# V kept per chunk and copied in one run per partition, with two full copy sets, a reused K buffer and a new order table

## Chip, cores and metric

One core of one Trainium2 chip. The metric is the device time of one launch in microseconds (us). Lower is better. Engines are called as in the profile: PE is the matmul engine, DVE, ACT and POOL are the vector, scalar and GpSimd engines, SP is the one that issues nearly all DMAs of both kernels. Four runs of the kernel before lay between 215.65 and 216.56 us; runs marked slow (over 1.5% above the fastest of the same kernel) are left out of every ratio.

## The reference, cut to what matters

```python
# x: 1 x 2048 x 512 (S x D), H = 32 heads of 16, window of W = 8 keys at distance 2 (dil)
h = layernorm(x) * (1 + ca) + sa                     # sa, ca, ga, sb, cb, gb = silu(c) @ w_mod
q, k, v = split_heads(h @ wqkv)
logits[s, w] = q[s] . k[s - 2 w] * Dh**-0.5          # masked where s - 2 w < 0
o[s] = sum over w of softmax(logits)[s, w] * v[s - 2 w]
x = x + ga * (o @ wo)
h = layernorm(x) * (1 + cb) + sb
h = layernorm(h)                                     # then a two-layer MLP along the sequence
x = x + gb * transpose(gelu(h^T @ w1 + b1) @ w2 + b2)
```

The sequence is handled in five chunks of 2, 4, 4, 4 and 2 tiles of 128 rows. DVE multiplies q by shifted k and the attention weights by shifted v; PE sums the products with narrow 0/1 matrices.

## The kernel before

For the products with V the partition of an operand is (window group w4, head): 32 heads in each of four groups of 32 partitions, group w4 holding V shifted by 2 w4 rows. So V, which lies with (head, quarter of the head's dimensions dq) on its partitions, is copied four times within SBUF, by DMA. The kernel before keeps one V of the whole sequence and copies each chunk quarter by quarter:

```python
v_f = T([P, 4, PAD + S], BF, "v_f")                      # partition = 4 * head + dq
vD_r = ring(5, [P, 4 * (CM + 8)], BF, "vD")              # five buffers of one quarter (NVD = 5)
...
for dhi in range(4):                                     # a quarter
    s_ = _Slot("vd"); vds.append(s_)
    for w4 in range(4):                                  # a window group
        s0 = PAD - 8 - 2 * w4
        def dst(s_=s_, w4=w4):
            return vD_r[s_.i][32 * w4:32 * w4 + 32, 0:4 * (C + 8)].rearrange("p (d s) -> p d s", d=4)
        dma(dst, v_c[dhi::4, :, s0:s0 + C + 8], ...)     # 4 runs of 2 * (C + 8) bytes per partition, on SP
...
# product of quarter dq: waits for the four copies of that quarter
nc.vector.tensor_tensor(pv(), a2sb..., vD_r[s_v.i]..., op=ALU.mult)
```

All these copies, the DMA transposes of the normalised tiles (hT) and all loads are issued by one engine, SP, in the order of a table that is part of the kernel. The modulation rows (ga and so on, spread over all partitions) are made by PE: four matmuls of 512 columns each.

## Time and profile before

| | kernel before |
|---|---|
| median of 3 runs | 216.03 us (215.65 to 216.56) |
| span of the profiled run | 214.4 us |
| first query-key product on DVE | 20.2 us |
| last normalised tile (h3) | 149.1 us |
| DVE idle between these two | 7.5 us |
| PE from the last h3 to the end | the MLP's last 284 matmuls, 61.5 us |

How to read it: between the first product and the last h3 DVE sets the pace, with PE nearly full beside it (busy for 121.4 and 124.6 of 128.9 us); then PE alone (busy for 61.2 of 61.5 us). A microsecond in which DVE idles in the first of these stages moves the end by about one: between the changed kernel and v_quarter_bytes (section 6) this idle time differs by 15.8 us and the time by 15.75. DVE's idle time there is the span of the stage less the union of its instructions. The V copies appear in the list of DMA issues (buffer and source, queue, number of issues, KB of one, median us from issue to landing):

```profile
vD<-v_f SPq DMA_DIRECT2D x48, 130.0 KB, 7.4
...
vD<-v_f SPq DMA_DIRECT2D x32, 66.0 KB, 3.6
```

And the chain of work that ended last, by engine, is PE's:

```profile
PE 73%; DVE 15%; DMA 4%; issue 3%; ACT 1%; POOLq 1%; SPq 1%; DVEq 0%
```

### The profile page before, as it was taken

To read this page: it belongs to the slowest core of one execution; us is meant where nothing else is said; L and a number is where in the kernel's file an instruction comes from. 1 tells how busy PE (TensorE), PEld (TensorE's weight loads), DVE (VectorE), ACT (ScalarE), POOL (GpSimd) and SP (SyncE) were. 2 spreads that over 40 slices of the span, in tenths; PEclk is the share of its full clock that TensorE was granted. 3 is DMA by queue.
4 is the path that set the end of the run, shared out by engine and by line. 5 is a ranking of instruction groups with operands and counts; after the bars stand their busy time and mean duration, and the time that the engine had idled before them with its cause. 6 is when DMAs were issued, how large, how long until landed. Compare 5 with 4: busy or idle time off the path is not lost.

```text
span 214.4 us, 3880 instructions
## 1 busy us (share of the span) xinstructions
PE 201.8 (94%) x1453; PEld 99.9 (47%) x1475; DVE 168.1 (78%) x256; ACT 123.9 (58%) x270; POOL 24.2 (11%) x43
## 2 busy tenths in 40 slices
PE   7599999899999999999999999988999999999992
PEld 7479345335444447443443344333444444444451
DVE  3699999799999999999999789997854445544553
ACT  3548778658789989988857668886852000000000
POOL 6030709100000000000000034034000000000000
PEclk9958999999999999999999999999999999999998
DMA  5999974359999999999999886449879110111011
GB/s 170 355 351 333 206 210 101 90 124 161 148 130 134 134 137 311 134 131 135 223 272 207 220 222 174 127 97 321 203 181 249 49 45 28 54 49 49 24 49 50
DMA packets 54182, 34.24 MB, mean 160 GB/s; under 512 B 18452, under 2 KB 54164, under 8 KB 54164
## 3 DMA queue, kind: packets, MB, share of 16 engines
q1 hardware_dynamic: 54156, 34.00, 74.6%
q8 instruction: 11, 0.18, 0.4%
q14 instruction: 7, 0.06, 0.1%
q10 hardware_dynamic: 8, 0.00, 0.0%
HBM read 22.03 MB, written 2.10 MB: 113 GB/s over the span
## 4 chain that ended last, share of the span: by engine, by line
PE 73%; DVE 15%; DMA 4%; issue 3%; ACT 1%; POOLq 1%; SPq 1%; DVEq 0%
PE psS L238 69%; DVE st L238 4%; DVE h L238 4%; PE psL L238 4%; DVE big L238 4%; DMA xx<-in_A_x_dram 3%; DMA hT<-h 2%; DVE mv L238 1%; POOLq L1082 1%; DVE xx L238 1%; SPq L238 1%; DVE w_qkv L238 0%; ACT lv L238 0%; ACT o_sb L238 0%; ACT k_f L238 0%
## 5 line engine op out<-in xcount | busy, mean ns | idle before, releaser
L238 PE MATMUL psS<-h,wst 128*128 128x512 bf16 x216 | 50.9, 379 | 1.7 <-POOL h L238 1.2
L238 PE MATMUL psS<-hT,w_qkv 128*128 128x512 bf16 (+1 forms) x234 | 47.1, 346 | 1.2 <-DMA hT<-h 0.9
L238 PEld LDWEIGHTS <-wst 128*128 128x128 bf16 x324 | 30.3, 99 | 35.4 <-issue 4.1
L238 PEld LDWEIGHTS <-w_qkv 128*128 128x128 bf16 x282 | 29.8, 114 | 23.7 <-issue 5.8
L238 DVE TENSOR_TENSOR big<-a2sb,vD 128x4096 bf16<-128x4096 bf16 (+1 forms) x20 | 37.0, 1863 | 2.0 <-DMA vD<-v_f 1.5
L238 DVE TENSOR_TENSOR big<-q_sb,k_f 128x4096 bf16<-128x4096 bf16 (+1 forms) x20 | 36.8, 1859 | 0.2 <-ACT k_f L238 0.2
L238 DVE SCALAR_TENSOR_TENSOR h<-psS,bcol,gb_bc 128x512 f32<-128x512 f32 (+1 forms) x17 | 12.2, 719 | 24.6 <-PE psS L238 24.5
L238 ACT ACTIVATE gT<-psS 128x512 bf16<-128x512 f32 x28 | 15.9, 591 | 5.2 <-PE psS L238 5.2
L238 PE MATMUL psS<-gT,big 128*128 128x512 bf16 x83 | 18.2, 379 | 0.1
L238 DVE BATCH_NORM_STATS2 st<-xx 128x6 f32<-128x512 bf16 x21 | 14.2, 675 | 4.2 <-DMA xx<-in_A_x_dram 4.1
L238 PE MATMUL psS<-woq,o_sb 128*128 128x512 bf16 x61 | 16.2, 380 | 0.2
L238 PE MATMUL psS<-gT,wst 128*128 128x512 bf16 (+1 forms) x83 | 15.3, 343 | 0.1
L238 PEld LDWEIGHTS <-big 128*128 128x128 bf16 x116 | 9.2, 98 | 12.3 <-DMA big<-in_w_mod_dram 2.4
L238 ACT ACTIVATE h<-xx,nb,rs 128x512 bf16<-128x512 bf16 x17 | 13.3, 809 | 1.8 <-DVE nb L238 1.7
L238 PEld LDWEIGHTS <-ident 128*128 128x128 bf16 (+1 forms) x146 | 11.1, 110 | 6.8 <-issue 1.7
L238 POOL TENSOR_SCALAR h<-xx,mv,rs 128x512 bf16<-128x512 bf16 x2 | 4.3, 2132 | 87.5 <-DVE xx L238 87.0
L238 ACT ACTIVATE q_sb<-psS,qvb 128x512 bf16<-128x512 f32 (+1 forms) x20 | 11.7, 605 | 4.0 <-PE psS L238 3.9
L238 DVE TENSOR_TENSOR psS<-psS,gT 128x512 f32<-128x512 f32 x14 | 9.2, 695 | 4.6 <-PE psS L238 4.6
L238 ACT ACTIVATE v_f<-psS,qvb 128x512 bf16<-128x512 f32 (+1 forms) x20 | 11.5, 601 | 1.1 <-PE psS L238 0.7
L238 POOL TENSOR_SCALAR h<-xx,rs,nb 128x512 bf16<-128x512 bf16 x7 | 10.3, 1485 | 15.3 <-DMA woq<-in_A_wo_dram 8.6
L238 ACT ACTIVATE k_f<-psS 128x512 bf16<-128x512 f32 x16 | 9.5, 597 | 4.0 <-PE psS L238 3.7
L238 ACT ACTIVATE lv<-mv,epscol 128x1 f32<-128x1 f32 (+2 forms) x25 | 7.3, 292 | 7.9 <-DVE mv L238 5.7
(96 smaller groups left out, 234.9 us busy)
## 6 DMA issues: line engine op xcount, KB each, us to landing
vD<-v_f SPq DMA_DIRECT2D x48, 130.0 KB, 7.4
wst<-in_B_w_dram SPq DMA_DIRECT2D x6, 768.0 KB, 5.6
wst<-in_B_w_dram SPq DMA_DIRECT2D x4, 896.0 KB, 5.8
big<-in_B_w_dram SPq DMA_DIRECT2D x3, 896.0 KB, 6.3
vD<-v_f SPq DMA_DIRECT2D x32, 66.0 KB, 3.6
out_dram<-h SPq DMA_DIRECT2D x15, 128.0 KB, 1.7
xx<-in_A_x_dram SPq DMA_DIRECT2D x3, 512.0 KB, 9.7
gT<-in_w_mod_dram SPq DMA_DIRECT2D x3, 512.0 KB, 9.4
```

The lines of the kernel that those rows point to most:

```text
L238: r = fn(*a, **k)
L1082: with _tile.TileContext(nc) as tc:
```

## The change

The intent: 20 issues of V copies instead of 80, each with one long run for each partition and quarter; V in two buffers of one chunk instead of a whole-sequence tensor (and K's buffer used twice), which frees SBUF; two full sets of copies instead of five quarters; fewer changes between wide and narrow matmuls by a new order table; PE busy with filler matmuls at the start. The modulation rows are made by 64 one-column matmuls, transposed, stored to DRAM and read back to all partitions. Cut to its core:

```diff
-    NVD: int = 5,
+    NVD: int = 2,
...
-    v_f = T([P, 4, PAD + S], BF, "v_f")
+    v_r = ring(2, [P, 4 * (CM + PAD)], BF, "v_sb")
...
-    vD_r = ring(NVD, [P, 4 * (CM + 8)], BF, "vD")
+    vD_r = ring(NVD, [P, 4, 4 * (CM + PAD)], BF, "vD")
...
-        for dhi in range(4):
-            s_ = _Slot("vd")
-            vds.append(s_)
-            for w4 in range(4):
-                s0 = PAD - 8 - 2 * w4
...
-                dma(dst, v_c[dhi::4, :, s0:s0 + C + 8], 32 * 4 * (C + 8) * 2,
...
+        s_ = _Slot("vd")
+        for w4 in range(4):
+            def f_vd(s_=s_, w4=w4):
+                n_ = 4 * (C + PAD) - PAD + 8
+                v_ = v_c[:, 0, PAD - 8 - 2 * w4:PAD - 7 - 2 * w4]
+                nc.sync.dma_start(vD_r[s_.i][32 * w4:32 * w4 + 32, :, 0:n_],
+                                  bass.AP(v_.tensor, v_.offset, [[v_.ap[0][0], P], [1, n_]]))
...
+            dma(lambda scr=scr: scr.rearrange("r (t p) -> (r t) p", p=P), rows, ...)      # rows to DRAM
+            dma(lambda r0=r0, nr=nr: rows_bc[:, r0:r0 + nr, :], ... scratch ...)          # and back, to all partitions
... (new order table; MLP sweeps cut at other tiles; normalisations on other engines)
```

Each product with V now waits for all four copies of its chunk, 2.1 MB in a chunk of four tiles.

## The prediction

> **What bounds the kernel now.** I read the busy shares first, then busy time by stage, then the chain that ended last, then the waits.
>
> ```profile
> PE 201.8 (94%) x1453; PEld 99.9 (47%) x1475; DVE 168.1 (78%) x256; ACT 123.9 (58%) x270; POOL 24.2 (11%) x43
> ...
> PEclk9958999999999999999999999999999999999998
> ```
>
> PE looks full, but the clock line shows two slices at half and 0.8, between 10.7 and 21 us. I therefore cut the span where the work changes: 20.2 us is the first query-key product on DVE, 149.0 us the last normalised tile (h3).
>
> ```profile
> core 0: us, PE busy (x) PEld busy (x) DVE busy (x) ACT busy (x) POOL busy (x), PEclk, DMA share, GB/s
> 2.90:20.20 17.30, 14.61 (x189) 12.88 (x188) 14.05 (x45) 9.41 (x21) 3.34 (x11) 0.80 1.06 339
> 20.20:143.40 123.20, 119.58 (x940) 54.38 (x955) 116.51 (x152) 99.91 (x225) 16.64 (x10) 1.00 0.93 168
> 143.40:149.00 5.60, 4.92 (x23) 2.15 (x23) 4.79 (x13) 3.46 (x10) 2.21 (x2) 1.00 1.05 287
> 149.00:210.50 61.50, 61.22 (x293) 29.05 (x297) 31.81 (x47) 9.88 (x15) 0.00 (x0) 1.00 0.35 93
> ```
>
> From 20.2 to 149 PE and DVE are both nearly full (DVE 121.3 of 128.8 us), so this stage has two bounds. After 149 us only PE matters: 284 matmuls of 512 columns are left (60 of the first MLP layer, 224 of the second), 61.5/284 = 0.2167 us each. What starts the tail is in the timeline:
>
> ```profile
> 146.77 2.17 POOL L238 TENSOR_SCALAR h<-h,mv,rs 128x512 bf16<-128x512 bf16 x1 [3.33 <-ACT rs L238]
> ...
> 148.99 5.34 PE L238 MATMUL psS<-h,wst 128*128 128x512 bf16 x23 [0.60 <-POOL h L238]
> ```
>
> The last normalisations stand on the slow POOL. What the change's title attacks, the shifted copies of V, costs almost nothing in waits; of the DVE's waits (us in total, times, longest):
>
> ```profile
> DVE h L238 <- PE psS L238: 24.5, 16, 2.4
> ...
> DVE big L238 <- DMA vD<-v_f: 1.5, 1, 1.5
> ```
>
> One more loss is hidden inside "busy" PE: changing between full-array and 32-column matmuls.
>
> ```profile
> 57.24 0.38 PE L238 MATMUL psS<-xx,ident 128*128 128x512 bf16 x1
> 57.55 0.62 PE L238 MATMUL psL<-big,group 128*32 128x512 bf16 x8
> 58.09 1.04 PE L238 MATMUL psS<-woq,o_sb 128*128 128x512 bf16 x4
> ```
>
> Four narrow matmuls run abreast, so eight should take 2 x 0.216 = 0.43 us; from start to next start they take 0.54. The plain one before them takes 0.31 instead of 0.216. Over all such groups the median loss is 0.115 us per switch.
>
> [...]
>
> **The change part by part.** The operations below are counted from the built order of both kernels; durations are those of before.
>
> 1. V copies: 80 issues become 20, 8.35 MB become about 8.7 MB. SP issues 60 x 0.606 = 36 us less, but SP bounds nothing. Worth at most the 1.5 us wait. Two full sets of V copies are enough: each set is rewritten two chunks later.
>
> 2. PE work. Removed: 16 matmuls of 512 columns for the modulation rows (3.5 us), 7 re-injections (1.5). Added: 64 one-column matmuls (16 take 0.55, so 2.2), two tiny transposes, one identity matmul (0.2), 90 filler matmuls early, outside the critical work, and a last output tile cut in three rather than two. Mode switches fall from 78 to 48: 30 x 0.115 = 3.5 us. Without fillers PE does about 6 us less. Between the first reduction and the first MLP matmul the old PE sum is 69.1 us, and before really took about 69 us there: PE was the bound. The new sum is 65.3.
>
> 3. DVE from the first query-key product to the last h3, by start-to-start times (2.20 us for a 4096-element product, 1.14 for 2048, 0.80 for a pair of statistics instructions, 0.32 for a normalisation, 0.73 for a residual add from PSUM): before 121.1 us, after 114.6. The differences: five statistics pairs moved in front of the stage (-4.0); three second-layernorm pairs moved to ACT (-2.4); about six normalisations moved to POOL or ACT (-2.0); one residual add gone (-0.7); three more mean/variance pairs (+1.4); a query eviction, small columns and the like (+1.2). The products of 74 us stay as they are.
>
> 4. In front of that stage DVE gets 17.4 us instead of 13.0. Where does the stage start? PE begins with the transposed c (needs its load, about 2.9 us like the first x tile), then 94 identity matmuls, half of them at 0.099 and half at 0.063: to 10.5. Then in PE's order 16 one-column products and 8 transposes (to 11.6), 36 fillers (13.8), 16 products (14.3), 11 fillers, two groups of transposes and one bias group: about 16.3. The key group is the fifth of 0.88 us, with a bias group between: 21.1; its eviction 0.6: the first product at **21.8** against 20.16. The fuller start keeps the clock up, which repays the half-rate stretch of 11 to 18 us; otherwise it would be later still.
>
> 5. Tail. The new sweeps of the first MLP layer leave 91 + 224 = 315 matmuls after the last h3, against 284: 68.3 us against 61.5. This is +6.8 us that the middle must win back. In exchange the last h3 is on DVE, not behind POOL. The final piece of 128 columns saves about 0.3 of the 3.9 us after the last matmul.
>
> 6. ACT loses about 5 us (ten parkings, row evictions, against three more square/sum passes); it is no bound. POOL gains seven normalisations of 1.5 to 2.1 us.
>
> Sum: 21.8 + 114.6 = 136.4, plus the DVE's idle time in the stage. Before it was 128.9 - 121.1 = 7.8 us, mostly waiting for PE and, at the end, in the layernorm chain with POOL. With 3.8 us less PE work up to the first MLP matmul and the rebuilt end, but with more POOL norms in the way of the affine steps, I choose 3.0. Then h3 ends at 139.4; + 0.3 hand-over + 68.3 = 208.0; + 3.6 = a span of 211.6; the measured time is 216.03 - 214.4 = 1.6 above the span: **213.2 us**, 1.3% faster. PE's own sum agrees: first MLP matmul about 93.6 (21.8 + 67.4 of DVE work + some idle and one POOL normalisation), then 110 us of PE work, gives 203.6 plus idle.
>
> **Rivals.** (a) *The order table works as meant and DVE has nearly no idle time.* Then 210.2 us, 2.7% faster. For it: fewer mode switches, statistics drawn forward into idle DVE time, woq's modulation placed 37 us of DVE work after the stage's start. Against it: no stage of before was free of waits, and the table fixes an order that cannot adapt. (b) *POOL turns into the wait.* Tiles 0, 2, 3 and 4 of the second layernorm are now normalised there; two in a row at 2.1 us cover more than the 2.7 us of DVE work put between the second group's coefficients and its affine step. Two or three such waits of 1 to 2 us give 214 to 216. (c) *A DMA takes over.* The modulation rows now go through DRAM on the same queue as the V copies; a wait of the queue for the first store holds up transposes and copies behind it. The old V copies landed in a median of 7.4 us, and the DMA share was about 1.1 from 50 to 120 us. If the woq step or a V product waits 4 us, 217. (d) *The longer tail is not won back*: idle time as before, 218.0.
>
> **Range and chances.** The time is 210.2 plus the DVE's idle time in the stage, plus or minus 1 for the start. Idle times of 0.5 to 6.5 give 210 to 217 (209.5 with an early start). Faster by over 2% means under 211.7, that is under 1.5 us idle: 0.33. Slower by over 2% needs 10 us: 0.07.
>
> **What would show it.** The first query-key product near 21.8 and the clock full from 8 us on; DVE idle 3 us between it and the last h3, near 139.4; DVE there 114.6 us busy; a PE tail of 68 us; the V copies' rate unchanged near 130 GB/s; no DVE wait on V copies over 2 us. Wrong would be: a tail shorter than 66 us, a first product before 20, a stage bounded by PE (DVE idle over 8 us), or a clock that falls in the middle.

The sum: 21.8 + 114.6 + 3.0 + 0.3 + 68.3 + 3.6 + 1.6 = 213.2. In the kernel before the first 36 identity matmuls took 3.57 us (0.099 each) and the next 25 took 1.57 (0.063); part 4 takes its two figures from them, and that half of the 94 would be slow is an estimate. PE was busy for 3.04 us from 5 to 10 us, and the granted clock was 0.50 from 11.2 to 18.0. POOL's normalisations of one tile took 1.49 to 2.13 us in the mean of their groups against 0.81 on ACT. For an unchanged rate of the V copies with longer runs no run was at hand. As for part 4's fuller start, in the changed kernel PE was busy for 14.0 of the 14.4 us from 8 us to the first product, at a clock of 1.00.

## The result, and the profile after

The changed kernel took **227.07 us** (median of 4 runs, 226.34 to 229.14) against 216.12 for the kernel before beside it: ratio 1.0523, 95% interval 1.045 to 1.0596, slower. A ratio here is the mean time of one kernel's fast runs over that of the other's fast runs of the same rounds, so it is not quite the ratio of the medians.

| | before | predicted | after |
|---|---|---|---|
| first query-key product | 20.16 | 21.8 | 22.36 |
| DVE busy from there to the last h3 | 121.4 | 114.6 | 114.5 |
| DVE idle in between | 7.5 | 3.0 | **17.8** |
| last h3 | 149.1 | 139.4 | 154.7 |
| from there to the end of the span | 65.3 | 72.2 | 70.9 |
| span | 214.4 | 211.6 | 225.6 |

Three of the four terms came out within 1.3 us. The idle time did not. Busy time, clock and chain of waits of the changed kernel:

```profile
PE 206.9 (92%) x1623; PEld 107.3 (48%) x1623; DVE 166.2 (74%) x262; ACT 117.1 (52%) x267; POOL 24.0 (11%) x52
...
PEclk9999999998599999998599999999999999999999
...
PE 52%; DMA 18%; DVE 15%; ACT 4%; SPq 3%; issue 2%; DVEq 0%
```

DVE is less busy than before (168.1 us), as intended. But DMA now holds 18% of the chain that ended last, where it had held 4%, and the clock falls to half twice in the middle. The same two stretches of both kernels, first before, then after (from and to, length, busy us and instructions of PE, PEld, DVE, ACT and POOL, granted clock, DMA share, GB/s):

```profile
50.00:60.00 10.00, 9.95 (x104) 4.57 (x103) 9.95 (x6) 8.16 (x17) 0.00 (x0) 1.00 1.09 147
80.00:110.00 30.00, 29.05 (x231) 14.84 (x232) 29.09 (x45) 25.99 (x67) 0.00 (x0) 1.00 1.15 187
```

```profile
50.00:60.00 10.00, 6.54 (x67) 2.51 (x67) 3.96 (x4) 2.94 (x7) 0.00 (x0) 0.74 1.08 117
80.00:110.00 30.00, 21.82 (x204) 12.79 (x203) 21.88 (x34) 20.03 (x52) 5.12 (x7) 0.93 1.05 176
```

From 50 to 60 us PE, DVE and ACT do less (PE is busy for 6.54 us of the 10, DVE for 3.96) while the DMA engines are as busy as before (1.08 against 1.09) but move less, 117 GB/s against 147. DVE's own timeline after the change has these gaps (start, length, engine, line, operation, operands, count, and in brackets the idle time in front and what the profile thinks ended it):

```profile
60.23 4.53 DVE L131 TENSOR_TENSOR big<-a2sb,vD 128x4096 bf16<-128x4096 bf16 x2 [6.28 <-PE psS L131]
...
85.09 4.49 DVE L131 TENSOR_TENSOR big<-a2sb,vD 128x4096 bf16<-128x4096 bf16 x2 [3.56 <-DMA vD<-v_sb]
...
99.57 1.42 DVE L131 TENSOR_TENSOR h<-h,rows_bc 128x1024 bf16<-128x1024 bf16 x2 [4.12 <-DMA rows_bc<-scratch]
...
118.25 2.29 DVE L131 TENSOR_TENSOR big<-a2sb,vD 128x4096 bf16<-128x4096 bf16 x1 [1.43 <-PE psS L131]
```

Together 15.4 of the 17.8 us. The first and last are put down to PE, but the trace shows the true cause of the first: the last V copy of chunk 1 was issued at 44.47 us and landed at 60.05 us, just before the product began. The product waits for several semaphores, and the label names one of them only. The DMA issues show how long the copies are under way:

```profile
vD<-v_sb SPq DMA_DIRECT2D x12, 526.0 KB, 16.5
...
vD<-v_sb SPq DMA_DIRECT2D x8, 270.0 KB, 7.3
```

The long copies take 16.5 us from issue to landing in the median. The packet records of the trace say that it is not only size: summed over the 16 engines, all V packets took 67.4 us of their time against 57.6 before, the 4208-byte runs moving at 122 GB/s where the 1040-byte runs of before moved at 133. PE, too, waits behind them: a transpose of hT issued at 43.08 landed at 55.48, and the clock was at half from 54.7 us on for 6.8 us.

```profile
55.53 6.81 PE L131 MATMUL psS<-hT,w_qkv 128*128 128x512 bf16 x17 [3.32 <-DMA hT<-h]
```

And SP, which issues everything in order, stands in front of the read-back of a modulation row until its store has landed; nothing goes out between 52.7 and 60.3 us:

```profile
50.36 0.31 SPq L131 DMA_DIRECT2D scratch<-mrows  x1
...
52.03 0.62 SPq L131 DMA_DIRECT2D woq<-in_A_wo_dram  x1
60.30 0.36 SPq L131 DMA_DIRECT2D rows_bc<-scratch  x1
60.76 1.24 SPq L131 DMA_TRANSPOSE hT<-h  x1
62.10 3.93 SPq L131 DMA_DIRECT2D vD<-v_sb  x4
```

So the suspects are: the *form* of the copies (their rate), the *coarse wait* (a product waits for all of a chunk), the *shared queue* (small urgent transfers behind big ones), the way of the rows through DRAM, and the new order itself.

### The profile page after: what moved, and what is told of

Its sections match the earlier page's. It is cut to its first block, busy times and chain, and to the rows that moved or that the text cites. A ratio compares the mean times of both kernels' runs of the same rounds, so it can differ in the third digit from the quotient of the medians.

```text
span 225.6 us, 4131 instructions
## 1 busy us (share of the span) xinstructions
PE 206.9 (92%) x1623; PEld 107.3 (48%) x1623; DVE 166.2 (74%) x262; ACT 117.1 (52%) x267; POOL 24.0 (11%) x52
## 3 DMA queue, kind: packets, MB, share of 16 engines
q1 hardware_dynamic: 47644, 34.65, 77.4%
## 4 chain that ended last, share of the span: by engine, by line
PE 52%; DMA 18%; DVE 15%; ACT 4%; SPq 3%; issue 2%; DVEq 0%
PE psS L131 51%; DVE big L131 6%; DMA hT<-h 5%; DMA rows_bc<-scratch 5%; DVE h L131 5%; DMA vD<-v_sb 4%; DMA scratch<-mrows 3%; SPq L131 3%; DVE st L131 2%; ACT h L131 2%; DVE mv L131 1%; DVE lsb L131 1%; PE psL L131 1%; ACT k_f L131 1%; ACT lv L131 0%
## 5 line engine op out<-in xcount | busy, mean ns | idle before, releaser
L131 PE MATMUL psS<-h,wst 128*128 128x512 bf16 x224 | 53.1, 389 | 0.0
L131 DVE SCALAR_TENSOR_TENSOR h<-psS,bcol,rows_bc 128x512 f32<-128x512 f32 (+2 forms) x18 | 12.4, 690 | 23.4 <-PE psS L131 23.2
L131 POOL TENSOR_SCALAR h<-xx,rs,nb 128x512 bf16<-128x512 bf16 x13 | 12.4, 960 | 72.3 <-DVE nb L131 69.8
L131 PEld LDWEIGHTS <-ident 128*128 128x128 bf16 x230 | 16.8, 110 | 4.6 <-issue 1.3
L131 PE MATMUL psS<-gT,wst 128*128 128x512 bf16 (+2 forms) x98 | 15.3, 318 | 0.0
L131 DVE TENSOR_TENSOR h<-h,rows_bc 128x512 bf16<-128x512 bf16 (+2 forms) x20 | 12.0, 600 | 4.5 <-DMA rows_bc<-scratch 4.1
L131 DVE BATCH_NORM_STATS2 st<-xx 128x6 f32<-128x512 bf16 x18 | 12.1, 674 | 4.1 <-DMA xx<-in_A_x_dram 4.1
L131 ACT ACTIVATE lv<-mv,epscol 128x1 f32<-128x1 f32 (+2 forms) x25 | 7.3, 294 | 13.8 <-DVE mv L131 13.5
L131 ACT ACTIVATE gT<-psS,bcol 128x512 bf16<-128x512 f32 x14 | 9.0, 684 | 10.3 <-DVE psS L131 10.1
L131 PE MATMUL psS<-ident 128*128 128x128 bf16 x168 | 13.0, 249 | 0.6 <-ACT a2sb L131 0.6
L131 ACT ACTIVATE v_sb<-psS,qvb 128x512 bf16<-128x512 f32 (+1 forms) x20 | 11.4, 596 | 4.0 <-PE psS L131 3.9
## 6 DMA issues: line engine op xcount, KB each, us to landing
vD<-v_sb SPq DMA_DIRECT2D x12, 526.0 KB, 16.5
```

The source lines that it names most:

```text
L131: r = fn(*a, **k)
```

## The experiments

All times are medians; every ratio is against runs of the kernel before on the same chip. "Idle" is DVE's idle time from the first query-key product to the last h3.

### 1. Take the copies away: v_copies_small

```diff
+    for t_ in vD_r:
+        nc.vector.memset(t_[:], 0.0)
...
-                n_ = 4 * (C + PAD) - PAD + 8
+                n_ = 264
```

> The changed kernel with each copy of V cut from 2104 (or 1080) to 264 elements a run, so that nearly all of the V copies' transfer time is gone while their number, order and waits stay; wrong result on purpose (the rest of both sets is zeroed on DVE before the first tile lands, which may push DVE's start by some 0.5 to 1 us). If the V copies, by whatever way, are the whole cause of the DVE's 17.6 us of idle time between the first query-key product and the last h3: idle falls to about 3 us, the time to 213 +- 2. If the modulation rows' way through DRAM or POOL or the new order itself is the cause: the wait of 4 us for the rows stays and the time is 220 or more.

Measured: 216.43 us, ratio 1.0011 (0.9974 to 1.0048). The idle time fell from 17.8 to 1.7 us and the wait for the rows was gone, but the zeroing delayed DVE's first product to 28.5 us, 6.2 us late. So the time itself says little, the stage much. (The comparison with the reference called this kernel correct: its tolerance does not see a damaged attention term.)

### 2. Finer waits, still one run a partition: by_quarter

```diff
-                nc.sync.dma_start(vD_r[s_.i][32 * w4:32 * w4 + 32, :, 0:n_],
-                                  bass.AP(v_.tensor, v_.offset, [[v_.ap[0][0], P], [1, n_]]))
+                for w in range(4):
+                    v_ = v_c[dq::4, 0, PAD - 8 - 2 * w:PAD - 7 - 2 * w]
+                    nc.sync.dma_start(vD_r[s_.i][32 * w:32 * w + 32, dq, 0:n_],
+                                      bass.AP(v_.tensor, v_.offset, [[v_.ap[0][0], 32], [1, n_]]))
...
-                    [("vD", ch, w4) for w4 in range(4)], frees=s_v, ...
+                    [("vD", ch, dq)], frees=s_v, ...
```

> The changed kernel with one run per partition kept, but the copies cut by quarter of the head dimensions (16 per chunk, issued in the order in which the products use them), each product waiting for its own quarter only, as in the kernel before; bytes and queue unchanged. Theory coarse wait (a product waits for all 2.1 MB of a chunk's copies where before it waited for a quarter): the DVE's gaps of 6.3, 3.6 and 1.4 us in front of the first V products vanish, the wait of 4.1 us for the modulation rows stays, time about 216 to 218. Theory shared queue (urgent small transfers stand behind V copies): those waits stay, gain under 3 us, time 224 to 227. Theory form (long runs copy slower): as good as nothing, 226 to 227.

Measured: 218.04 us, ratio 1.0076 (1.0032 to 1.0119); idle 8.3 us. The gain fits the coarse-wait theory's number, but the reason was not the one stated: the packets themselves ran faster, 4208-byte runs at 208 GB/s instead of 122, and the row wait vanished with them. One gap of 5.8 us was left, in front of which PE had waited for hT (and then ran at half clock for 6.8 us):

```profile
56.28 7.79 PE L131 MATMUL psS<-hT,w_qkv 128*128 128x512 bf16 x24 [3.54 <-DMA hT<-h]
```

### 3. The old form: short_runs

```diff
-                nc.sync.dma_start(vD_r[s_.i][32 * w4:32 * w4 + 32, :, 0:n_], ...)
+                for dhi in range(4):
+                    nc.sync.dma_start(vD_r[s_.i][32 * w4:32 * w4 + 32, dhi, 0:4 * (C + PAD)].rearrange(
+                        "p (d s) -> p d s", d=4)[:, :, 0:C + 8], v_c[dhi::4, :, PAD - 8 - 2 * w4:PAD - 2 * w4 + C])
```

> The changed kernel with the V copies in the old form: 80 copies of 32 partitions with four short runs (1040 or 528 bytes) instead of 20 with one run of 4208 or 2160 for each partition and quarter; same waits (a product waits for the whole set), same queue. Theory form: the copies take some 58 us of the 16 DMA engines instead of 67, the sets land about 2 us earlier each, the time falls by 3 to 6 us to 221 to 224, and the rate of their packets is 133 GB/s or more. Theories coarse wait and shared queue: SP issues 60 more copies at 0.6 us, nothing lands earlier by over 1 us, 225 to 229.

Measured: 221.10 us, ratio 1.0227 (1.0177 to 1.0276); idle 10.0 us; packets of 1040 bytes at 138 GB/s. As the form theory said, at its upper end: 80 copies in four short runs beat 20 in one long run by 6 us, with the same coarse wait and 60 more issues on SP. But with the old form back it is still 5.0 us above the kernel before, and DVE still waits for V copies twice, 4.1 us in all.

### 4. Other queues for the urgent transfers: urgent_own_queues

```diff
-                dma_t = lambda sl=sl, st=st: nc.sync.dma_start_transpose(out=hT[:, :, sl * P:(sl + 1) * P],
+                dma_t = lambda sl=sl, st=st: nc.scalar.dma_start_transpose(out=hT[:, :, sl * P:(sl + 1) * P],
... (and the rows' store and read-back by nc.gpsimd.dma_start)
```

> The changed kernel with the small urgent transfers taken out of the queue of the V copies: the DMA transposes of hT issued from ACT, the modulation rows' store to DRAM and broadcast back issued from POOL. Theory shared queue: the PE's wait for hT (3.3 us at 52 us) and the DVE's wait for the rows (4.1 us) vanish, the PE clock does not fall at 55 us, and with SP no longer standing in its order behind the transposes the V copies are issued earlier too: 217 to 221. Theory coarse wait: the gaps of 6.3, 3.6 and 1.4 us stay, only the row wait goes or shrinks: 222 to 225. Theory bandwidth (V copies take all the write bandwidth, whatever the queue): the small transfers take as long as before beside them, 225 or more.

Measured: 236.64 us, ratio 1.0955 (1.0887 to 1.1024); idle 24.9 us: worse by 9.6 us than the changed kernel, which no theory had said. The rows, from POOL's queue, were no faster where V copies were under way: the read-back of the second group landed 15.7 us after its issue, against 11.1 in the changed kernel. (The first group met no V copies here and landed in 3.4 us, against 5.2.) DVE's wait:

```profile
DVE h L131 <- DMA rows_bc<-scratch: 12.2, 1, 12.2
```

And ACT was held by the transposes that it now had to issue. Usually an issue takes 1.2 us; with V copies in flight two took 4.5 and 7.0 us (ACT's queue in the timeline), and ACT's evictions stood behind them:

```profile
40.91 1.21 ACTq L131 DMA_TRANSPOSE hT<-h  x1
...
42.19 4.48 ACTq L131 DMA_TRANSPOSE hT<-h  x1
...
46.79 7.02 ACTq L131 DMA_TRANSPOSE hT<-h  x1
```

So a queue of its own did not shorten the rows' read-back beside V copies (15.7 us against 11.1); how long the transposes themselves took from issue to landing was not read. The bandwidth theory's "225 or more" held. How the loss divides is not shown: DVE's wait for the second rows grew from 4.1 to 12.2 us, and ACT's stall stood in front of two other gaps of DVE, 2.8 and 4.7 us.

### 5. The copies alone: copy_rates

A kernel that only copies x to the output and then moves one chunk's set of V copies (2.1 MB) in each form, phase by phase.

> Not the kernel but its V copies alone (result wrong on purpose: the output is x): all shifted copies of one 512-column chunk, once in each form, one phase at a time, each phase ended by a DVE read of all of it. Forms: as changed (4 copies of 32 partitions, 4 runs of 4208 bytes into one partition one after another), as before (16 copies, 4 runs of 1040 into each partition), by quarter (16 copies, one run of 4208 a partition), the first and third with the window groups in the order 0, 2, 1, 3, the first over two queues, and each with a load of 0.9 MB of W1 ahead. If what slows the copies is that one copy writes several runs into the same partition one after another: the changed form takes about 16 us (131 GB/s), the old one about 16, by quarter about 10.5 (16 issues at 0.65 us bound it). If the form makes no difference and by quarter was quicker in the kernel only because fewer other transfers were in flight: all three take 10 to 11 us or all 16. [...]

Measured from the landing times in its trace, copies back to back and nothing else under way:

| form | us from one landing to the next | GB/s |
|---|---|---|
| as changed: 128 partitions into 32, 4 runs of 4208 bytes each | 4.57 for 538.6 KB | 118 |
| as before: every fourth partition, 4 runs of 1040 bytes | 0.94 for 133.1 KB | 142 |
| by quarter: every fourth partition, 1 run of 4208 bytes | 0.79 to 0.86 for 134.7 KB | 157 to 170 |

A set of 2.1 MB is thus 18.3 us as changed (4 x 4.57), 15.0 as before (16 x 0.94), 12.6 to 13.8 by quarter. The order of the window groups made no difference (alternating: 4.6 and 0.86 us), two queues next to none (20.0 us from the first issue to the last landing, against 20.5); the alternative that is cut had expected these two to save a third or more of the changed form. The trace also shows issues that stand still until an earlier copy has landed: SP issued at 129.62, 134.25 and 138.74 us, each within 0.02 us of the landing of one of the long copies (129.61, 134.23, 138.72). The loads of W1 did not land beside the copies as planned and tell nothing. So the changed form is the slowest of the three by itself; "by quarter was quicker only because less else was in flight" is out.

### 6. The floor, measured cleanly: v_quarter_bytes

```diff
-                n_ = 4 * (C + PAD) - PAD + 8
+                n_ = C + 8
...
-                    _ap(vD_r[s_v.i][:, dq, 8:9], [[-8, 2], [C + PAD, 4], [1, C]]), op=ALU.mult)
+                    _ap(vD_r[s_v.i][:, dq, 8:9], [[-8, 2], [0, 4], [1, C]]), op=ALU.mult)
```

> The changed kernel with each copy of V cut to its first 520 elements a run (a quarter of the bytes), the products reading these four times over; number, order, queue and waits as changed; result wrong on purpose. This is the small-copy run without its zeroing on DVE, which had pushed the first query-key product from 22.4 to 28.5 us. If the V copies' time is the whole of the miss: first product at 22.4, DVE idle 1 to 2 us up to the last h3, 210 to 212 us. If the late start had only given the other transfers time to come in: idle 4 us or more, 214 or more.

Measured: **211.32 us** (210.79 to 211.44), ratio 0.9775 (0.9745 to 0.9805). First product 22.56, idle 2.0 us, last h3 138.6, clock full throughout. From its page (its long copies now hold 130 KB and land after 5.0 us instead of 16.5):

```profile
PEclk9999999999999999999999999999999999999999
...
vD<-v_sb SPq DMA_DIRECT2D x12, 130.0 KB, 5.0
```

With a quarter of the V copies' bytes, and everything else of the change in place (order, DRAM rows, POOL normalisations, one queue), the kernel is 2.3% faster than before. Rows, order and POOL are thus no causes by themselves; without the V copies' bytes the whole of the miss is gone.

### 7. Rate or wait: quarter_coarse

```diff
-                    [("vD", ch, dq)], frees=s_v, ...
+                    [("vD", ch, w4) for w4 in range(4)], frees=s_v, ...
```
(against by_quarter)

> The by-quarter copies (16 per chunk, one run a partition), but each product waits for all 16 of its chunk as in the changed kernel. Theory coarse wait: the gain of by quarter (9 us of 227) is lost again, 224 or more. Theory rate (the copies of the changed form are slow, the wait for all of them does not matter by itself): under 220, within 1 to 2 us of by quarter's 218.

Measured: 218.57 us, ratio 1.0114 (1.0062 to 1.0166); idle 8.4 us. With these copies, waiting for the whole set costs 0.5 us or nothing. The rate theory holds: 8.5 of the 11 us come back with the copies' form alone. What the coarse wait costs when the copies are slower was not run.

### 8. SP's issues shared with ACT: quarter_two_queues

```diff
-                    nc.sync.dma_start(vD_r[s_.i][32 * w:32 * w + 32, dq, 0:n_],
+                    (nc.scalar if w > 1 else nc.sync).dma_start(vD_r[s_.i][32 * w:32 * w + 32, dq, 0:n_],
```
(against by_quarter)

> By quarter, with the copies of window groups 2 and 3 issued from ACT's queue, so that SP issues 8 instead of 16 per chunk and the transposes of hT behind them in SP's order go 5 us earlier. In by quarter the one big gap of DVE left is 5.8 us at 59 us, behind the PE, which waited for hT at half clock. If SP's issue time caused it: gap under 2 us, clock full throughout, 212 to 215. If ACT's evictions are held up by its 8 issues per chunk (some 5 us, as the transposes held it up in the run with own queues): 217 or more.

Measured: 238.50 us, ratio 1.1038 (1.1007 to 1.1069); idle 28.5 us. The second alternative, and much stronger than expected. On ACT's queue two V copies together took up to 3.45 us to issue (from 70.29 us) where one had taken 0.50 (at 41.24), and the eviction behind them waited 5.67 us, put down to a V copy. In all, ACT's waits of this kind in front of q's evictions were (us, times, longest):

```profile
ACT q_sb L131 <- DMA vD<-v_sb: 6.6, 2, 5.7
```

### 9. Transposes first: quarter_xt_first and xt_first

The order table only, and in it only SP's part: `xt11` (a transpose of hT) moves up behind `xt10`, `vd1_1` (the second group of chunk 1's V copies) down behind `xt13`; once with the by-quarter copies, once with the changed kernel's own.

> By quarter (16 copies per chunk, one run a partition, each product waiting for its own quarter), and in SP's order the last transposes of hT for chunk 3 go ahead of the second and third group of chunk 1's V copies; nothing else. In the by-quarter run the only big gap of DVE (5.8 us at 59 us) is the PE's wait for that hT (3.5 us) and the half clock of 6.8 us after it. If the order on SP is the cause: clock full from 54 to 61 us, DVE idle 2 to 3 us in the stage, 212 to 214, faster than the kernel before by 1 to 2%. If the V copies then come too late for the first products of chunk 1: a gap of 2 us or more at 52 to 60 us on V copies, 215 to 217.

Measured: 217.86 us, ratio 1.0088 (1.0067 to 1.0109); idle 7.2 us. The clock stayed full and PE's wait was gone, as said, but the time did not move. Another wait had taken its place, with the same end:

```profile
64.90 1.23 DVE L131 TENSOR_TENSOR woq<-woq,rows_bc 128x2048 bf16<-128x2048 bf16 x1 [4.86 <-DMA rows_bc<-scratch]
```

> The changed kernel with its own slow copies and only that reordering on SP. If it is the order of the one queue that costs (urgent transfers behind V copies): the 6.3 us gap at 54 us shrinks by 3 us or more and the time is 222 to 224. If the slow copies themselves cost: they land as late as before (60 us), the gap stays at 5 us or more, 225 to 228.

Measured: 225.45 us, ratio 1.0420 (1.0387 to 1.0454); idle 13.8 us, the gap at 54 us now 7.0. The copies' answer, in time (225 to 228) and in the gap (5 us or more).

### 10. What makes a copy slow: copy_rates_2

> Copies alone again (output x, wrong on purpose), 2.1 MB a phase, to find what in the changed form is slow; in the first such run it moved 117 GB/s, the old form 140, by quarter 163. If it is several rows written into one partition by one copy: two rows a partition lies between 117 and 163, blocks of 32 neighbouring partitions run like quarter (about 163), block_short like the old form (140). If it is the read of 128 neighbouring partitions: block is as slow as changed (117 to 130). If short or unaligned rows matter: aligned is over 180. [...]all over 250 GB/s, with all_short slower than all by as much as short rows cost.

Measured from landing to landing, alone:

| form | us per copy | GB/s |
|---|---|---|
| changed: 128 partitions into 32, 4 rows each | 4.51 for 538.6 KB | 119 |
| two_rows: 64 neighbours into 32, 2 rows each | 2.02 for 269.3 KB | 133 |
| quarter: every fourth of 128 into 32, 1 row | 0.86 for 134.7 KB | 157 |
| block: 32 neighbours into 32, 1 row | 0.64 for 134.7 KB | 210 (SP's issue pace, 16 in 10.10 us) |
| aligned: as block, 4096 bytes from a row's start | 0.67 for 131.1 KB | 196 (SP's pace) |
| block_short: 32 neighbours, 4 runs of 1040 bytes | 0.68 for 133.1 KB | 195 (SP's pace) |
| all: 128 partitions into the same 128, 1 row | 1.30 for 538.6 KB | 413 |
| all_short: the same, 4 runs of 1040 | 1.48 for 532.5 KB | 360 |

DVE's waits from the end of the phase before it to the end of these phases (leftovers of another form, two small copies, lie in front of the second and third):

```profile
65.19 0.17 DVE L63 COPY mark<-vDquarter 128x8 bf16<-128x8 bf16 x1 [15.92 <-DMA vDquarter<-v_sb]
...
77.57 0.17 DVE L63 COPY mark<-vDblock 128x8 bf16<-128x8 bf16 x1 [12.00 <-DMA vDblock<-v_sb]
...
128.44 0.17 DVE L63 COPY mark<-vDchanged 128x8 bf16<-128x8 bf16 x1 [20.46 <-DMA vDchanged<-v_sb]
```

Neither of my two hypotheses stands. Four runs into one partition are not slow (block_short keeps SP's pace), and reading 128 partitions is not slow (all: 413 GB/s; the 250 expected for it was an estimate). The length of a run matters little (360 against 413); its alignment shows nothing at SP's pace (196 against 210), so a small effect would not be seen. What the slow ones have in common, a pattern in these eight forms and not yet a cause, is that the partitions read and the partitions written do not run side by side: four rows of neighbours folded into one partition (119), two (133), every fourth (157). Why copies into the same 32 partitions run at 119 and 157 where neighbours reach 210 no run here shows; it stays open.

### 11. Rows first: quarter_rows_first and rows_first

In SP's order, beside the move above: the two late quarters of Wo with the first two, the row's store before the last two groups of chunk 1's copies, its read-back before the last one.

> By quarter; on SP the transposes of hT for chunk 3 stand before most of chunk 1's V copies, the store of the first modulation row before chunk 1's last two groups and its broadcast before the last one, and the two late quarters of Wo are loaded with the first two. If the order of the urgent transfers on SP is what is left: the 4.9 us wait for the row vanishes, DVE idle in the stage 1.5 to 3 us, 212 to 214, 1 to 2% faster than the kernel before. If the copies themselves are still the limit: a gap of 2 us or more on V copies takes its place, 215 to 218.

Measured: 215.67 us, ratio 0.9993 (0.9969 to 1.0017); idle 5.8 us. The row wait vanished and 2.2 us were won, less than expected: a third wait came up. ACT wanted to write V of chunk 3 into the buffer of chunk 1 and waited for the last copy out of it; DVE then waited 3.5 us behind ACT and PE.

```profile
60.62 0.69 ACT L131 ACTIVATE v_sb<-psS,qvb 128x512 bf16<-128x512 f32 x1 [5.01 <-DMA vD<-v_sb]
```

> The changed kernel's own four copies per chunk with the same order on SP. If the order alone was at fault in the changed kernel: under 218. If the copies' rate is: the V products of chunk 1 still wait until all 2.1 MB are in, at 58 us or later, and 222 to 226.

Measured: 226.09 us, ratio 1.0460 (1.0427 to 1.0493); idle 16.6 us, the gap in front of chunk 1's V products 8.4 us. With the slow copies the better order is worth 1 us, which is within the noise of the two ratios. Order by itself was not at fault in the changed kernel.

### 12. Fewer issues: mixed_rows_first

```diff
+                if ch in (0, 4):
+                    ... one copy of 128 partitions per window group, as changed
+                    return
```

> As quarter_rows_first, but the small chunks 0 and 4 copied in the changed form (4 issues instead of 16 each, at 119 GB/s): SP has 8 us less to issue before chunk 1. If the number of issues on SP still costs: 0.5 to 1.5 us better than quarter_rows_first. If not, the same within 0.5, or worse by up to 1 us where chunk 0's first product waits for all four copies.

Measured: three fast runs from 215.21 to 216.22 (ratio 0.9989, 0.9958 to 1.0019), three slow ones at 219, and the profile fell into the slow ones, so I read no waits from it. On time alone: the same as quarter_rows_first. As far as three runs tell, the number of issues on SP is not what is left.

### 13. Buffer, layout, and both: quarter_ring3, block_rows_first, block_ring3

```diff
-    v_r = ring(2, [P, 4 * (CM + PAD)], BF, "v_sb")          # quarter_ring3, block_ring3
+    v_r = ring(3, [P, 4 * (CM + PAD)], BF, "v_sb")
...
+            if t == 2:                                         # block_*: V's weight columns reordered when scaled
+                d_ = d_.rearrange("p (j q h) -> p j q h", j=4, q=4)
+                s_ = s_.rearrange("p (h q j) -> p j q h", j=4, q=4)
...
-                    v_ = v_c[dq::4, 0, PAD - 8 - 2 * w:PAD - 7 - 2 * w]
+                    v_ = v_c[32 * dq:32 * dq + 32, 0, PAD - 8 - 2 * w:PAD - 7 - 2 * w]
... (the bias columns of V in the same order)
```

> As quarter_rows_first with a third buffer for V, so that chunk 3's V need not wait for the copies of chunk 1. If the wait on the buffer is what is left: ACT's 5.0 us at 60 us and the DVE's 3.5 us at 64 us go, DVE idle 1.5 to 2.5 us, 212 to 213.5. If another wait takes its place again: 214.5 to 216.

Measured: 215.79 us, ratio 0.9985 (0.9952 to 1.0019); idle 5.7 us. The buffer wait is gone, and in its place stands a fourth one: 3.7 us for the second group of modulation rows at 85 us.

> As quarter_rows_first, but the columns of the V weights are put in another order when they are scaled, so that a quarter of V lies in 32 neighbouring partitions; the copies (16 per chunk, one run a partition) read neighbours instead of every fourth partition; two V buffers as before. If the reading of every fourth partition holds the copies back: they land every 0.65 us instead of every 0.85, packets of 4208 bytes at 280 GB/s or more instead of some 200, chunk 1's last copy lands 3 us earlier, ACT's wait shrinks to 2 us or less, 212.5 to 214.5; the scaling of V's weights may cost up to 1 us at the start. If not: 215.5 to 217.

Measured: 215.87 us, ratio 0.9985 (0.9960 to 1.0011); idle 4.0 us. The copies were faster (median of a 4208-byte packet 304 ns against 429, over all 233 GB/s against 169), less so than I had said (280 or more), and the wait shrank from 3.5 to 1.1 us. (Packet rates differ between kernels: the same by-quarter copies made 208 GB/s in by_quarter, 169 in quarter_rows_first and 190 in quarter_ring3.) But the reordered scaling costs: with the strided read one tile's scaling took 0.97 us on DVE instead of 0.45, 1.24 on ACT instead of 0.71 and 1.42 on POOL instead of 0.70, and the first product came at 23.1 instead of 22.1 us.

> Both. If nothing else is in the way: at the floor, 211.5 to 213, 1.5 to 2% faster than the kernel before. If the start loses more by the reordered weights than the copies gain: 213 to 215.

Measured: **214.24 us** (fast runs 213.3 to 215.3, one slow run left out), ratio **0.9906** (0.9873 to 0.9939); idle 2.4 us, last h3 at 139.9 us, against 154.7 as changed. Its busy times and clock:

```profile
PE 201.1 (95%) x1671; PEld 105.0 (50%) x1671; DVE 166.1 (79%) x262; ACT 117.2 (55%) x267; POOL 31.2 (15%) x52
...
PEclk9999999999999999999999999999999999999999
```

This version beats both kernels: 0.9% faster than before (clear of noise), and some 6% faster than as changed (214.24/227.07 = 0.943, a ratio of medians from different chips). In a simulation, its output, like quarter_ring3's, was the same to the last bit as the changed kernel's. It is 2.9 us from the floor; the two profiled spans differ by 2.0 us (211.6 against 209.6), of which the later first product is 1.3 (23.83 against 22.56) and the end 0.7.

## Why the prediction was wrong, point by point

The sum was right and one term of it was not.

- **First product at 21.8**: 22.36. Right within 0.6 us, with the clock full from 7 us on, until 54.7.
- **DVE busy 114.6**: 114.5. Right.
- **DVE idle 3.0, "I choose 3.0"**: 17.8. This is the step that failed, and it carries the whole miss: 22.4 + 114.5 + 3.0 + 70.9 = 210.8, close to the predicted span of 211.6. v_quarter_bytes shows 2.0 us of idle time where the copies weigh little, and 211.32 us, almost at my rival (a) of 210.2 without any idle time.
- **"V copies ... Worth at most the 1.5 us wait"** is why the term was mis-sized. I looked up what the old copies cost in waits and concluded that new ones could only save. I did not ask what happens if the new ones are slower. They were: 118 GB/s alone where the old form does 142, so the set of a four-tile chunk takes 18.3 us of the DMA engines alone, out of the 29 us in which DVE works through such a chunk (114.5 us for 16 tiles), and the transposes, the rows and the loads of W1 go through the same queue (q1, 77.4% of the 16 engines' span in the changed kernel).
- **"The V copies' rate unchanged near 130 GB/s"**: in the kernel 122 (4208-byte runs) against 133 (1040-byte runs), and over all V packets 129 against 148. The prediction assumed that the length of the runs does not matter, and no run had shown it. For these lengths it held within 13% (360 against 413 GB/s, over 128 partitions). The wrong step was to read it as "so the form does not matter". The form changed which partitions are read beside which are written, and between copies into 32 partitions with and without that change the rate differed by a factor of 1.8 or more (119 against 210, which is SP's pace).
- **Rival (c), "A DMA takes over ... 217"**: the mechanism happened, several of its waits in a row (V products, hT in front of PE, rows). The size I gave it, one wait of 4 us, was under a third of the 14.8 us of additional idle time that came. I had its best evidence in hand: a DMA share of 1.15 from 50 to 120 us in the kernel before. A resource that is full before the change is not one on which to book "no cost".
- **Rival (b), POOL becomes the wait**: no. One tile's normalisation on POOL took 0.96 us in the mean, not 1.49 to 2.13, and none of DVE's gaps over 0.4 us is put down to it.
- **Fewer mode switches, tail of 68 us, last h3 on DVE**: as told (from 20 to 160 us PE changes 50 times between full-array and 32-column matmuls, against 80 before); from the last h3 to the end it took 70.9 us where I said 72.2.
- **"A clock that falls in the middle"** was named as a sign of being wrong, and it was there, twice for 6.83 us. It was a consequence: in v_quarter_bytes it does not fall. Both falls came during or just after a PE wait (3.32 us for hT, 2.90 us put down to ACT), after 4 us in which PE had been busy for 1.44 and 0.93.
- **Figures that do not hold as written**, though none moves the result: the old copies move 8.55 MB, not 8.35 (the profile's KB are 1024 bytes); two or three waits of 1 to 2 us in rival (b), on top of 3.0, give 215 to 219 and not 214 to 216; and the profiled run took 216.15, so the time is 1.75 and not 1.6 above the span.

What was shown: the V copies' transfers are the cause (v_quarter_bytes), and their rate is the main part of it (quarter_coarse gives back 8.5 of the 15.8 us to the floor). With the by-quarter copies the coarse wait costs nothing clear of noise; with the slow ones order alone is worth 1 to 2 us. But quarter_coarse copies faster than the kernel before did. With the old form (short_runs) 6.0 us come back and 5.0 us against the kernel before remain; how these divide between the coarse wait at that rate, 60 more issues and the rest of the change was not separated. What came after the rate was a queue of waits: hT, the row through DRAM, the V buffer, the second rows. Mending any one of them moved the wait to the next with a gain of 0 to 2.2 us. Only faster copies and a third buffer together ended it. Not settled: why a copy that folds four partitions into one is slow, and how much of the time the two falls of the clock cost by themselves.

## What to carry to other kernels

Count a copy by which partitions it reads and writes, not by its issues and run lengths, and measure its rate alone before building an order on it: of the three forms that the kernel could use as it stood, the one with the fewest issues, and runs as long as any, was the slowest (118 GB/s against 142 and 157 to 170). When the DMA engines are already full (a share of 1.15 from 50 to 120 us here), an edit that touches their traffic has no "worth at most": price it as bytes over a measured rate against the time that the consumers leave. And where removing a wait changes nothing, look for the next wait on the same resource before calling the cause disproved.
